# First batch loaded as float32 and cast on chip, denominators ahead of numerators, ordered loads: an attention and feed-forward kernel

## The chip, the cores and the metric

The kernel runs on one core of one Trainium2 chip. The metric is the device time of one execution in microseconds (us); the median of several executions is given. The profile shows one execution; its span, from the first instruction to the last, is 1.7 to 2.0 us shorter than the timed value of the same execution. Engines: TensorE (PE in the profile, with its weight loads as PEld), VectorE (DVE), ScalarE (ACT), GpSimd (POOL) and SP. SP computes nothing and only issues transfers. "ACTq" and "SPq" are the transfers that ScalarE and SP issue.

## The reference

```python
# q, k, v: (8 batches, 8 heads, 576 tokens, 64)
scores = scale * q @ k.T                       # heads 0..3: sliding window of 32
scores = where(masks, scores, -1e9)            # heads 4..7: window of 128, every 4th token
attn = exp(scores - max) / (sum + 1e-9)
x = (attn @ v) laid out as (4608 tokens, 512)
g = x @ w_gate; val = x @ w_val                # 512 -> 1536
out = (gelu(g) * val) @ w_out                  # 1536 -> 512, float32
```

## The kernel before

The feed-forward part goes over 9 chunks of 512 tokens. Each chunk has a first layer (12 blocks of 128 hidden columns, 96 matmuls) and a second half (four tiles of 128 tokens, 48 matmuls, each tile copied and stored). The attention of later batches is woven in. A batch has four units of two heads each (two plain, two dilated): scores on TensorE, an exponential on ScalarE, a mask on VectorE, products with v ("numerators") and with ones ("denominators") on TensorE, then a normalisation in four VectorE steps (transpose, reciprocal, transpose, product into `xT`).

```python
# all q, k, v and weights: casting transfers (float32 -> float16) issued by GpSimd
def load_qk(b):                                   # 14 transfers on GpSimd ...
    for kb in range(5):
        for t, src in ((0, q), (1, k)):
            nc.gpsimd.dma_start(out=qp[0:n, kb, t], in_=...)
    # ... then 7 transposes by DMA, on SP
    nc.sync.dma_start_transpose(out=dst[...], in_=...)
...
# head: batch 0, numerators and denominators of a unit together
for i in range(1, 4):
    emit_s(i, SB, pe_mask=True)
    pv_all(i - 1, 1)                              # products, then the four VectorE steps
pv_all(3, 1)
...
# chunk 0's second half does the scores of batches 1 and 2 and the products of batch 1;
# chunk c from 1 on does the products of batch c+1 and the scores of batch c+2
...
def store(c, tb, bank, eng):
    nc.scalar.activation(osb, ps[:, bank, :], AF.Copy, ...)   # or VectorE
    nc.scalar.dma_start(out=out[t0 : t0 + P, :], in_=osb)     # every store: issued by ScalarE
```

The softmax here doesn't subtract the row's maximum and nothing guards it: scores larger than these inputs give would overflow.

## Time and profile before

| | before |
|---|---|
| time, median (3 runs) | 375.63 us (374.6 to 377.14) |
| span of the profile | 372.9 us, mean granted TensorE clock 0.972 |
| head, to the first first-layer matmul that had to wait | 37.1 us |
| chunk 0: first layer, second half | 21.5 and 26.8 us |
| chunk 1, chunk 2 | 38.9 and 37.0 us |
| the rest | 211.6 us |

The rest is TensorE back to back and moves in no run of this study by more than a microsecond unless a wait lies in it. So, such waits apart, only the first 161 us can gain or lose. The lines behind the table are in the prediction. A line of a timeline has: start, length, engine, line of the program, operation, result<-operands, how many, and in brackets the idle time of the engine before it with what ended that.

### The profile page before, as it was taken

How to read it: one execution, taken by the hardware profiler on the slowest of the kernel's cores; microseconds unless marked ns; L12 is line 12 of the kernel's file. 1: busy time of each engine (PE TensorE's matmuls, PEld its weight loads, DVE VectorE, ACT ScalarE, POOL GpSimd, SP SyncE). 2: the span in 40 equal slices, each digit the busy share in tenths (PEclk: the TensorE clock that was granted, in tenths of full speed). 3: DMA queues.
4: the chain of work that ended last, by engine and by line, in shares of the span. 5: the costliest groups of instructions: out<-in, count | busy, mean ns of one | idle time of the engine just before them, and what ended most of it. 6: DMA issues, size and time to landing. Idle time of an engine off the chain costs nothing.

```text
span 372.9 us, 6286 instructions
## 1 busy us (share of the span) xinstructions
PE 341.8 (92%) x2556; PEld 164.5 (44%) x2556; DVE 196.6 (53%) x285; ACT 144.4 (39%) x204; POOL 120.2 (32%) x175
## 2 busy tenths in 40 slices
PE   1664998959999999999999999999999999999996
PEld 0442443534444444444444444444444444444442
DVE  2356233775973497359725972596269603312420
ACT  2441234445236523652364336434642213313321
POOL 7924947759598657239100000000000000000000
PEclk9996799977999999999999999999999999999999
DMA  9999999999999999989417101100110020011002
GB/s 136 149 206 184 166 207 144 218 203 173 169 139 203 173 161 99 155 170 108 45 59 163 21 2 56 58 0 2 58 57 2 0 86 29 0 58 56 0 28 87
DMA packets 113229, 37.55 MB, mean 101 GB/s; under 512 B 88768, under 2 KB 108480, under 8 KB 113200
## 3 DMA queue, kind: packets, MB, share of 16 engines
q0 software_dynamic: 75440, 19.15, 55.1%
q1 hardware_dynamic: 32576, 8.56, 16.2%
q10 hardware_dynamic: 5184, 9.44, 6.9%
q8 instruction: 20, 0.33, 0.4%
q14 instruction: 9, 0.07, 0.1%
HBM read 38.57 MB, written 9.44 MB: 129 GB/s over the span
## 4 chain that ended last, share of the span: by engine, by line
PE 83%; DVE 11%; ACT 2%; DMA 2%; issue 1%; POOL 0%; DVEq 0%; POOLq 0%
PE ps L433 46%; PE ps L444 25%; PE ps L393 7%; DVE xT L416 3%; DVE dt L398 2%; DVE rb L402 2%; PE ps L310 2%; PE ps L293 2%; DMA qm_first<-in_k_dram 2%; DVE u L438 1%; ACT P L296 1%; DVE rc L400 1%; DVE qTp L208 1%; PE ps L282 1%; DVE osb L457 1%
## 5 line engine op out<-in xcount | busy, mean ns | idle before, releaser
L437 ACT ACTIVATE g<-ps 128x512 f16<-128x512 f32 x108 | 64.0, 597 | 143.2 <-PE ps L433 143.2
L433 PE MATMUL ps<-xT,wg 128*128 128x512 f16 x432 | 114.0, 387 | 1.8 <-DVE xT L416 1.8
L433 PE MATMUL ps<-xT,wv 128*128 128x512 f16 x432 | 112.8, 384 | 0.0
L438 DVE SCALAR_TENSOR_TENSOR u<-g,ps 128x512 f16<-128x512 f16 x108 | 73.9, 688 | 71.2 <-PE ps L433 57.3
L444 PE MATMUL ps<-wo,u 128*128 128x512 f16 x432 | 98.4, 380 | 1.2 <-DVE osb L457 1.2
L433 PEld LDWEIGHTS <-wv 128*128 128x128 f16 x432 | 42.7, 99 | 54.7 <-issue 5.0
L433 PEld LDWEIGHTS <-wg 128*128 128x128 f16 x432 | 40.7, 99 | 49.4 <-issue 3.2
L444 PEld LDWEIGHTS <-u 128*128 128x128 f16 x432 | 40.2, 98 | 48.7 <-issue 1.5
L166 POOL DMA_DIRECT2D qp<-in_q_dram x35 | 25.7, 735 | 14.4 <-DMA wg<-in_moe_w_gate_dram 4.1
L166 POOL DMA_DIRECT2D qp<-in_k_dram x35 | 25.8, 736 | 13.9 <-DMA qd<-in_k_dram 4.3
L398 DVE STREAM_TRANSPOSE dt<-ps 128x576 f32<-128x576 f32 x32 | 25.1, 783 | 9.5 <-PE ps L393 6.2
L317 DVE TENSOR_TENSOR P<-P,mask_p 128x1440 f16<-128x1440 f16 x14 | 12.7, 908 | 27.9 <-ACT P L297 27.9
L312 ACT ACTIVATE P<-ps 128x1280 f16<-128x1280 f32 x16 | 19.8, 1237 | 17.7 <-PE ps L310 15.6
L455 ACT ACTIVATE osb<-ps 128x512 f32<-128x512 f32 x26 | 15.5, 597 | 26.2 <-PE ps L444 26.2
L402 DVE STREAM_TRANSPOSE rb<-rc 128x576 f32<-128x576 f32 x32 | 24.9, 778 | 1.1
L189 POOL DMA_DIRECT2D vp<-in_v_dram x32 | 24.2, 792 | 2.6 <-DMA qp<-in_k_dram 1.6
L457 DVE TENSOR_SCALAR osb<-ps 128x512 f32<-128x512 f32 x10 | 6.9, 690 | 31.8 <-PE ps L444 31.8
L317 DVE TENSOR_TENSOR P<-P,mask_d 128x1280 f16<-128x1280 f16 x14 | 11.5, 824 | 17.6 <-ACT P L312 17.6
L296 ACT ACTIVATE P<-ps 128x800 f16<-128x800 f32 x16 | 13.4, 837 | 14.6 <-PE ps L293 14.5
L416 DVE TENSOR_TENSOR xT<-ps,rb 128x576 f16<-128x576 f32 x16 | 18.0, 1124 | 0.1
L393 PE MATMUL ps<-P,ones 128*64 128x64 f16 (+4 forms) x320 | 15.7, 228 | 0.0
L393 PE MATMUL ps<-P,vd 128*64 128x144 f16 x128 | 8.7, 242 | 6.1 <-DVE xT L416 4.4
(61 smaller groups left out, 203.3 us busy)
## 6 DMA issues: line engine op xcount, KB each, us to landing
out_dram<-osb ACTq DMA_DIRECT2D x36, 256.0 KB, 2.0
vp<-in_v_dram POOLq DMA_DIRECT2D x32, 64.0 KB, 4.6
vd<-in_v_dram POOLq DMA_DIRECT2D x8, 256.0 KB, 5.7
qd<-in_q_dram POOLq DMA_DIRECT2D x7, 256.0 KB, 8.3
qd<-in_k_dram POOLq DMA_DIRECT2D x7, 256.0 KB, 9.7
qp<-in_q_dram POOLq DMA_DIRECT2D x28, 64.0 KB, 5.4
qp<-in_k_dram POOLq DMA_DIRECT2D x28, 64.0 KB, 5.5
wg<-in_moe_w_gate_dram POOLq DMA_DIRECT2D x3, 512.0 KB, 10.2
```

The lines of the kernel that those rows point to most:

```text
L166: nc.gpsimd.dma_start(out=qp[0:n, kb, t], in_=src[b, 0:HK, kb * P : kb * P + n, :].rearrange("h p d -> p h d"),)
L189: nc.gpsimd.dma_start(out=vp[:, kb, :, :], in_=v[b, 0:HK, kb * P : (kb + 1) * P, :].rearrange("h p d -> p h d"),)
L312: nc.scalar.activation(pt, ps[:, b0 : b0 + 4, 0:DW], AF.Exp, bias=0.0, scale=scale)
L317: nc.vector.tensor_tensor(pt, pt, mb, ALU.mult)
L393: nc.tensor.matmul(o, lhs, rhs, start=st, stop=True, skip_group_check=True)
L398: nc.vector.transpose(dt.rearrange("p b c -> p (b c)"), den)
L402: nc.vector.transpose(rb.rearrange("p (b c) -> p b c", c=32), bass.AP(tensor=rc.tensor, offset=rc.offset, ap=[rc.ap[0], [1, 18], [0, 32]]),)
L416: nc.vector.tensor_tensor(dst.rearrange("p (i m s) -> p i m s", m=2, s=2), num, rb.rearrange("p (s m i) -> p i m s", s=2, m=2), ALU.mult,)
L433: nc.tensor.matmul(ps[:, b0 + gi, :], w[:, kc, ns], xT[kc][:, tok], start=(kc == 0), stop=(kc == NKC - 1))
L437: nc.scalar.activation(g, ps[:, b0, :], AF.Gelu)
L438: nc.vector.scalar_tensor_tensor(u_t[nb], g, USCALE, ps[:, b0 + 1, :], ALU.mult, ALU.mult)
L444: nc.tensor.matmul(ps[:, bank, :], u_t[fc][:, tb * P : (tb + 1) * P], wo_t[fc // 4][:, fc % 4, :], start=(fc == 0), stop=(fc == NNB - 1),)
```

## The change

It is meant to shorten the head and to take work from GpSimd and from chunk 0. The first batch comes as plain float32 transfers on SP and ScalarE and is cast on chip. The denominators of a unit go ahead of its numerators, and chunk 0's first layer starts on three of the four key chunks (slices of 128 of the 512 input columns, one from each unit of the attention). Batches 1 to 7 load plain q, k, v as float32 through SP, GpSimd casts them, and a staging pool of single buffers takes the place of double ones. Batch 1 is transposed on TensorE. Batch 1's loads are gated on a weight load, that is, made to wait until it has landed, and batch 2's on the last output weights. Batch 2's scores move from chunk 0 to chunk 1.

```diff
-    ldp = ctx.enter_context(tc.tile_pool(name="ldp", bufs=2))
+    ldp = ctx.enter_context(tc.tile_pool(name="ldp", bufs=1))
...
+    def load_qk_plain(b):                      # 10 transfers on SP, float32
+                gated(nc.sync.dma_start(out=st[0:n, kb, t], in_=sr))
+    def cast_qk_plain(b, st):
+        nc.gpsimd.tensor_copy(qp[:, 0:4], st[:, 0:4])
+        nc.gpsimd.tensor_copy(qp[0:64, 4], st[0:64, 4])
...                                             # v: 5 more transfers on SP, 2 casts
+    def load_batch(b):
+        st = load_qk_plain(b)
+        sv = new_v(b)
+        qd, rd = load_qk_dil(b)
+        qp = cast_qk_plain(b, st)
+        v_plain(b, sv, nc.sync)
+        crossbar(b, qp, qd, rd)                # 7 transposes on SP
+        load_v_dil(b)
+        v_cast(b, sv)
...                                             # head, first batch
+    emit_pv(0, V, ("den",))
+    norm_r(0, V)
...
+    emit_pv(1, V, ("den",))
+    norm_r(1, V)
+    emit_pv(0, V, ("num",))
+    norm_x(0, V)
...
+    gate["dma"] = w1
+    st1 = load_qk_plain(1)
+    qp1 = cast_qk_plain(1, st1)                # in GpSimd's order between load_wo(0) ...
+    load_wo(1)                                 # ... and load_wo(1), load_wo(2)
+    wo2 = load_wo(2)
...                                             # chunk 0
+            if c == 0 and nb == 8:
+                t_plain(1, qp1, 4, ("act", "act", "act", "act"))
+            if c == 0 and nb == 10:
+                gate["dma"] = wo2
+                load_batch(2)
```

## The prediction

> **What bounds the kernel now.** I read the slices and groups of the page first, then cut the span into stages, then walked the chain of waits, then looked at the granted clock, the DMA packets and ScalarE's order of work. By stages (from:to, length, busy us of the TensorE, its weight loads, VectorE, ScalarE, GpSimd, clock, DMA, GB/s):
>
> ```profile
> 0.00:37.10 37.10, 17.07 (x228) 11.41 (x229) 17.16 (x27) 12.62 (x16) 23.05 (x37) 0.92 1.29 169
> 37.10:58.60 21.50, 21.50 (x91) 9.25 (x91) 7.57 (x11) 6.61 (x12) 14.54 (x22) 0.90 1.54 188
> 58.60:85.40 26.80, 20.43 (x252) 11.11 (x250) 18.33 (x26) 12.47 (x15) 19.52 (x29) 0.88 1.68 187
> 85.40:124.30 38.90, 38.74 (x297) 18.07 (x294) 23.57 (x34) 18.00 (x24) 32.04 (x47) 0.95 1.79 168
> 161.30:372.90 211.60, 207.23 (x1405) 97.13 (x1402) 106.99 (x155) 78.02 (x115) 13.21 (x19) 1.00 0.23 49
> ```
>
> These are the head (first batch's attention), chunk 0 of the FFN in two halves, chunk 1, and the last stretch. From 124.3 us on TensorE runs back to back: 96 first-layer matmuls take 20.72 us and 48 second-layer ones 10.36 us in the chain, 0.216 us each, and the nine chunks' 279.7 us cannot shrink. Only the first 124.3 us can. There the chain of waits (start, length, what) is the normalisation, one VectorE step after another:
>
> ```profile
> 21.32 0.83 ACT P L296
> 22.16 0.79 DVE dt L398
> 22.97 0.28 DVE rc L400
> 23.27 0.79 DVE rb L402
> 24.08 0.77 DVE xT L413
> 24.89 0.84 PE ps L393 x20
> ...
> 35.91 1.14 DVE xT L416
> 37.09 21.44 PE ps L433 x89
> ```
>
> Four units pass in single file: numerators and denominators on TensorE (0.84), then four VectorE steps, and the next unit's products wait for the last step to free the bank. The clock in the two late stretches:
>
> ```profile
> 31.00:41.30 10.30, 7.04 (x37) 2.96 (x38) 5.06 (x7) 0.77 (x2) 7.19 (x10) 0.50 1.66 164
> 78.80:89.10 10.30, 7.52 (x75) 4.30 (x75) 6.32 (x9) 7.22 (x8) 8.44 (x12) 0.50 1.83 179
> ```
>
> Half speed, each time after some 3 us in which TensorE did little. One more wait, ScalarE's order near the end of chunk 0:
>
> ```profile
> 75.12 0.60 ACT L455 ACTIVATE osb<-ps 128x512 f32<-128x512 f32 x1 [0.80 <-PE ps L444]
> 78.42 0.34 ACTq L459 DMA_DIRECT2D out_dram<-osb  x1
> 78.80 0.84 ACT L296 ACTIVATE P<-ps 128x800 f16<-128x800 f32 x1 [3.08 <-PE ps L293]
> ```
>
> The tile to be stored was ready at 75.72, the store was issued at 78.42. By the program's own list of waits it reuses one of eight completion counters of the hardware queues, and that counter belonged to a transpose of batch 2 that landed at about 78.4. ScalarE waits in order, so everything behind the store waits too.
>
> **What the Trainium skill says.** "TensorE: Matmul & The Clock Gate", Part 1: the clock is at half until a window of about 3.4 us was busy, and falls back after an idle one. The trace agrees: the 0.50 stretches above, the second after a 2.28 us wait. "DMA: Bandwidth & Descriptors", SWDGE vs HWDGE vs iDMA: a casting DMA must come from GpSimd; SP and ScalarE issue plain ones. So float32 loads need a cast on chip. The trace agrees so far as all loads with a cast sit on GpSimd's queue, at some 0.75 us of GpSimd each, 5.9 us to the first landing. "GPSIMD Engine Reference", 3.1 Elementwise: one-input operations run near 1.03 cycles an element at 1.2 GHz. No trace here shows a cast; my estimate from that page is 0.9 us for 128x1024, 1.8 for 128x2048.
>
> **The change, part by part.**
>
> *Head.* Batch 0's plain q and k now come in 64-float rows, 4608 packets of 256 B. In the trace's packet records, 256 B packets of the hardware queue (ident's 128, and those of the transposes) take 18 ns in the median; over 16 engines that is 5.2 us. The first packet moved at 1.7 us, so they land at L = 7.5 to 10; I take 8.5. Before, the first transpose started at 7.20: nothing is gained in arrival. From L: cast 0.4, transposes 0.4, PSUM copy 0.65 (dense now, against 1.30 strided), bias and scores at half clock 1.6, exponentials 0.84 + 0.70, so the first P is there at L + 4.7. But the first denominators stand behind the dilated transposes, which need two GpSimd casts with two weight DMA issues (0.76 each) between them, after the dilated data (about L + 3.7): L + 8.6. From there VectorE is the bound: four times (0.79 + 0.28 + 0.79), two xT of 0.77 and two of 1.14, four small copies of 0.4: about 12.7. Denominators ahead of numerators remove the 0.84 of TensorE and the wait for it from each of three units. The third unit's xT, which frees the bank, ends at about L + 20.7. The first layer now starts with three of the four key chunks, so the last xT is hidden. Effective start of chunk 0: L + 20.3 = 28.8, against 36.4 before (37.09 less three matmuls done). **Gain 7.6.**
>
> *Chunk 0.* First layer 20.7, half clock at its start about 2.6 (before: 37.09 to 41.3 at half speed, 2.1), 52 transposes of batch 1 that moved from DMA to TensorE: 32 at 0.07 and 20 at 0.035, 2.9. The second half drops batch 2's four scores. FFN 10.4 + four scores at 0.44 + four products at 0.8 = 15.3, plus 2.6 at the end where two normalisations (3.0 each) run in series with 12 matmuls beside them: 17.9. Sum 44.4 against 49.0. **Gain 4.6**, if ScalarE is never held.
>
> *ScalarE held by its stores.* In the changed program's order the second store of chunk 0 takes the counter of the third plain transpose of batch 2, the third and fourth store those of q and k loads of batch 3, which SP issues only after all seven transposes of batch 2. Batch 2's loads wait for the last of wo (estimate 49 us from 15.9 us for six weight loads, 8.2 for wo, and the rest at the packet rates), its dilated loads for the transposes of batch 1 on TensorE (53.5). Transposes then run from about 59, at a pace of 2.0, 1.6 and 1.3 each and 3.5 to landing (the uncontended set at 158.7 us). The second store is ready at 62 and freed at about 69; the fourth, at 75. ScalarE's exponentials stand behind them. Worked through, chunk 0 ends 5.1 later. **Loss 0 to 5.1.**
>
> *Chunk 1.* First layer 20.7. Second half: FFN 10.4, eight scores 3.5, four products 3.2 = 17.1; but the last four scores share four banks and each waits for the exponentials of the one before (1.54 or 1.24 + 0.45), 7 us with little on TensorE: 21.9, and then a half clock stretch, 2.6, and about 1 at its start. Sum 46.2 against 38.9, which had only four scores. **Loss 7.3** (before, the same four scores cost this in chunk 0).
>
> *Rest.* Same matmuls, same order: 0. Plain loads go from 15 GpSimd issues a batch to SP, GpSimd casts 5 to 6 us a batch, off the path.
>
> Sum: -7.6 - 4.6 + 7.3 = -4.9 with ScalarE free; +0.2 or, with one more half clock stretch (1.6), +1.8 with ScalarE fully held. I put about half the weight on each: -1.6. Schedules this deliberate usually were tuned on the chip, so I lean 2 us further to the fast side: 372.0.
>
> **Rivals.** (1) ScalarE is held, all of the head's gain turns into a wait for batch 2's transposes: 377. For: the stalled store above, the order of the changed program. Against: the loads may be 5 us earlier than I think. (2) The head is better than worked (TensorE stays warm, loads land at 7.5, casts are quick) and no store is held: 365. For: DMA has less to do early, transposes of batch 1 left it; before, two waits on transposes cost 2.3 us. Against: VectorE's 12.7 us of chain remains. (3) Weights come late: the first weight load moves behind a GpSimd cast, to about 12 us, later ones behind four casts; slow casts of 2 us each would push wg1 and wo: 380. Against: before they went out at 13.2 to 17.6 too, and the layer now needs them at 28.
>
> **Range and chances.** 2% faster is 368.1: 4 us below my value, needing a free ScalarE and one more good turn: 0.32. 2% slower is 383.1, needing a held ScalarE and late weights: 0.13. Within: 0.55. Range 363.5 to 380.5 from rivals 2 and 3.
>
> **What would show it.** First matmul of the first layer near 27 to 29 us, VectorE nearly gapless from about 17; four normalisations spaced 2.7 to 3 us, not 3.6 to 4.6. Chunk 0's first layer ends near 55. A store issue on ScalarE long after its copy, with a score or an exponential late behind it, shows rival 1. Four scores in single file near 115 us and a clock of 0.50 after. From chunk 2 on, 37.0 us a chunk as before. It is wrong if dilated casts or loads hold the first denominators past 20 us, or if a first-layer matmul waits for weights.

## The result

The changed kernel takes 395.23 us (394.32 to 395.46, 4 runs) against 375.94 us for the kernel before in the same rounds. The ratio is 1.0509, with a 95% interval of 1.0469 to 1.055: slower. Ratios here are the mean time of one kernel's fast runs over that of the other's of the same rounds, so they are not quite the ratios of the medians. The spans are 393.5 and 372.9 us.

The stages of the changed kernel, in the same columns as in the prediction (from:to, length, busy us of TensorE, its weight loads, VectorE, ScalarE, GpSimd, clock, DMA, GB/s):

```profile
0.00:31.30 31.30, 21.32 (x233) 12.72 (x234) 15.06 (x33) 11.18 (x14) 13.06 (x21) 0.87 1.05 198
31.30:61.30 30.00, 26.10 (x149) 12.62 (x147) 9.41 (x13) 11.36 (x22) 8.62 (x12) 0.91 1.09 175
61.30:99.30 38.00, 24.20 (x213) 11.37 (x212) 14.98 (x21) 10.62 (x13) 13.22 (x17) 0.78 1.29 201
99.30:141.00 41.70, 37.85 (x334) 19.06 (x334) 19.96 (x29) 21.85 (x30) 10.19 (x15) 0.94 0.98 143
```

The head ends earlier. The next row, chunk 0's first layer, is 8.5 us longer than before (30.0 against 21.5), and in the third row, chunk 0's second half and the start of chunk 1, TensorE is busy 24.2 of 38.0 us at a clock of 0.78.

The head itself does what was meant. VectorE's first step of the four normalisations (`dt`) and the two last products:

```profile
19.69 0.78 DVE L422 STREAM_TRANSPOSE dt<-ps 128x576 f32<-128x576 f32 x1 [0.21 <-PE ps L417]
23.10 0.78 DVE L422 STREAM_TRANSPOSE dt<-ps 128x576 f32<-128x576 f32 x1
26.20 0.78 DVE L422 STREAM_TRANSPOSE dt<-ps 128x576 f32<-128x576 f32 x1 [0.56 <-PE ps L417]
29.30 0.78 DVE L422 STREAM_TRANSPOSE dt<-ps 128x576 f32<-128x576 f32 x1 [0.57 <-PE ps L417]
31.13 2.12 DVE L440 TENSOR_TENSOR xT<-ps,rb 128x576 f16<-128x576 f32 x2
```

They come every 3.1 to 3.4 us; before, the last two stood 4.6 us apart, and the last `xT` ended at 37.04 and not at 33.25.

ScalarE in chunk 0's second half:

```profile
65.23 0.60 ACT L495 ACTIVATE osb<-ps 128x512 f32<-128x512 f32 x1 [0.64 <-PE ps L484]
73.42 0.37 ACTq L499 DMA_DIRECT2D out_dram<-osb  x1
74.16 0.84 ACT L313 ACTIVATE P<-ps 128x800 f16<-128x800 f32 x1 [8.34 <-DMA sv<-in_v_dram]
...
85.41 0.36 ACTq L499 DMA_DIRECT2D out_dram<-osb  x1
85.82 1.24 ACT L329 ACTIVATE P<-ps 128x1280 f16<-128x1280 f32 x1 [9.73 <-DMA qTp<-qp]
```

The tile is ready at 65.83, its store goes out at 73.42, and the exponential behind it starts at 74.16. What ended the wait is a load of v of batch 2, which neither the tile nor the exponential uses. The second store waits 9.73 us for a transpose of batch 2. In the compiled program each of these stores reuses one of eight completion counters that SP's and ScalarE's transfers share, and the user of that counter before it is this load, or this transpose; ScalarE's wait for its landing stands right in front of the store. The third and fourth store wait likewise for a q and a k load of batch 3 and go out at 90.25 and 93.73.

And what the load and the transpose wait for, from the chain of waits that ended last (start, length, what):

```profile
23.28 7.53 DMA wv<-in_moe_w_val_dram
...
37.31 3.98 SPq L180
...
47.23 3.45 DMA sv<-in_v_dram
50.74 0.19 POOL wo L126
...
51.46 7.58 DMA wo<-in_moe_w_out_dram
59.10 0.37 SPq L180
...
69.84 3.69 DMA sv<-in_v_dram
...
78.03 7.30 DMA qTp<-qp
```

From 23 to 85 us the chain has no TensorE in it. A weight load opens the gate for batch 1's loads; they land at about 48; GpSimd, which casts them, can only then issue the last output weights; these open the gate for batch 2's loads; then come its casts, its transposes and the held store. The chain puts the issue of the weights down to a load of v that landed at the same moment. GpSimd's own timeline shows what stood in front of it:

```profile
48.33 1.89 POOL L185 CAST qp<-st 128x2048 f16<-128x2048 f32 x1 [18.97 <-DMA st<-in_k_dram]
50.16 0.61 POOL L186 CAST qp<-st 64x512 f16<-64x512 f32 x1
50.72 1.48 POOL L126 DMA_DIRECT2D wo<-in_moe_w_out_dram  x2
```

TensorE's matmuls wait for no transfer from 30 to 182 us: their waits in the profile's list are for ScalarE, VectorE and GpSimd, the longest 5.99 and 4.86 us, for the two held exponentials.

Three moments of TensorE compare the kernels: S0, the first score in chunk 0 (end of its first layer), S1, the first score in chunk 1, and S2, the issue of chunk 2's first store. S0 and S1 before, then after:

```profile
59.31 0.49 PE L293 MATMUL ps<-qTp 64*128 64x160 f16 x10
111.76 0.49 PE L293 MATMUL ps<-qTp 64*128 64x160 f16 x10
```

```profile
62.01 0.49 PE L310 MATMUL ps<-qTp 64*128 64x160 f16 x10
117.70 0.49 PE L310 MATMUL ps<-qTp 64*128 64x160 f16 x10
```

S2 before, then after:

```profile
152.58 0.34 ACTq L459 DMA_DIRECT2D out_dram<-osb  x1
```

```profile
173.39 0.34 ACTq L499 DMA_DIRECT2D out_dram<-osb  x1
```

| stretch | before | after | after less before |
|---|---|---|---|
| start to S0 | 59.31 | 62.01 | +2.70 |
| S0 to S1 | 52.45 | 55.69 | +3.24 |
| S1 to S2 (152.58 and 173.39) | 40.82 | 55.69 | +14.87 |
| S2 to the end (372.9 and 393.5) | 220.32 | 220.11 | -0.21 |

The table alone misleads about the place of the loss, because the change moved batch 2's scores from the second stretch into the third. The experiments separate this. Each row is read from one execution: in five traces whose programs are the same up to S0 (the changed kernel and the four runs below that only move its stores) S0 lies between 60.26 and 62.91, so the first row is good to about 2.7 us.

### The profile page after: what moved, and what is told of

It is laid out like the page before. It is cut to its first block, busy times and chain, and to the rows that moved or that the text cites. A ratio compares the mean times of both kernels' runs of the same rounds, so it can differ in the third digit from the quotient of the medians.

```text
span 393.5 us, 6470 instructions
## 1 busy us (share of the span) xinstructions
PE 354.8 (90%) x2616; PEld 170.9 (43%) x2616; DVE 195.2 (50%) x289; ACT 149.1 (38%) x215; POOL 66.6 (17%) x89
## 4 chain that ended last, share of the span: by engine, by line
PE 60%; SPq 15%; DMA 12%; DVE 7%; issue 2%; POOL 1%; ACT 1%; ACTq 0%; POOLq 0%; DVEq 0%
PE ps L452 31%; PE ps L484 21%; SPq L180 9%; SPq L214 4%; PE ps L417 3%; DMA sv<-in_v_dram 3%; DMA wo<-in_moe_w_out_dram 2%; DMA wv<-in_moe_w_val_dram 2%; DMA qTp<-qp 2%; DVE xT L440 2%; DVE dt L422 2%; DVE u_all L478 2%; PE ps L327 1%; SPq L168 1%; DVE rb L426 1%
## 5 line engine op out<-in xcount | busy, mean ns | idle before, releaser
L478 DVE SCALAR_TENSOR_TENSOR u_all<-g,ps 128x512 f16<-128x512 f16 x108 | 73.5, 686 | 80.8 <-PE ps L452 65.0
L452 PE MATMUL ps<-xT,wg 128*128 128x512 f16 x408 | 105.7, 382 | 0.1
L452 PE MATMUL ps<-xT,wv 128*128 128x512 f16 x408 | 104.7, 379 | 0.5 <-DVE u_all L478 0.5
L484 PE MATMUL ps<-wo,u_all 128*128 128x512 f16 x432 | 102.1, 391 | 0.0
L484 PEld LDWEIGHTS <-u_all 128*128 128x128 f16 x432 | 41.3, 100 | 50.6 <-issue 5.2
L452 PEld LDWEIGHTS <-wv 128*128 128x128 f16 x408 | 39.9, 98 | 49.2 <-issue 1.4
L452 PEld LDWEIGHTS <-wg 128*128 128x128 f16 x408 | 38.1, 98 | 45.7 <-issue 1.2
L185 POOL CAST qp<-st 128x2048 f16<-128x2048 f32 x7 | 13.2, 1890 | 86.9 <-DMA st<-in_k_dram 63.4
L327 PE MATMUL ps<-qTd 64*128 64x16 f16 (+1 forms) x256 | 9.9, 208 | 14.6 <-ACT P L313 7.4
L440 DVE TENSOR_TENSOR xT<-ps,rb 128x576 f16<-128x576 f32 x16 | 17.9, 1122 | 0.1
L417 PE MATMUL ps<-P,ones 128*64 128x64 f16 (+4 forms) x320 | 15.4, 226 | 1.9 <-DVE xT L437 1.9
L327 PEld LDWEIGHTS <-qTd 64*128 64x128 f16 x256 | 7.5, 100 | 19.6 <-issue 18.5
```

The source lines that it names most:

```text
L327: mm(o, kt[:, k0 : k0 + P], qt[:, q0:q1], start=st, stop=True, skip_group_check=True)
L417: nc.tensor.matmul(o, lhs, rhs, start=st, stop=True, skip_group_check=True)
L440: nc.vector.tensor_tensor(dst.rearrange("p (i m s) -> p i m s", m=2, s=2), num, rb.rearrange("p (s m i) -> p i m s", s=2, m=2), ALU.mult,)
L452: nc.tensor.matmul(ps[:, b0 + gi, :], w[:, kc, ns], xT[kc][:, tok], start=(kc == 0), stop=(kc == NKC - 1))
L478: nc.vector.scalar_tensor_tensor(u_all[:, nb, :], g, USCALE, ps[:, b0 + 1, :], ALU.mult, ALU.mult)
L484: nc.tensor.matmul(ps[:, bank, :], u_all[:, fc, tb * P : (tb + 1) * P], wo_t[fc // 4][:, fc % 4, :], start=(fc == 0), stop=(fc == NNB - 1),)
```

## The experiments

Theory: ScalarE, held by its own stores, is the loss; the stores wait for SP's late stream of loads and transposes. Rivals: TensorE itself lacks the data; the gates make everything late; the weights are late; later chunks lose by themselves. The first and the third are already weak, since TensorE's matmuls wait for no transfer there. The single buffers of the staging pool were not tested alone; in the changed kernel's trace SP waits for GpSimd 1.5 us in all.

Timed runs, each with the kernel before of the same rounds:

| run | us | before | ratio (95%) |
|---|---|---|---|
| stores of chunks 0 to 2 by GpSimd | 396.56 | 374.71 | 1.0569 (1.0523 to 1.0615) |
| no gates | 395.37 | 374.71 | 1.0537 (1.0482 to 1.0593) |
| both | 395.69 | 374.71 | 1.0555 (1.0494 to 1.0615) |
| casting loads for batches 1 to 7 | 385.32 | 374.71 | 1.0286 (1.0225 to 1.0346) |
| stores of chunk 0 by GpSimd | 391.62 | 375.68 | 1.0429 (1.038 to 1.0478) |
| same, numerators with denominators | 394.34 | 375.68 | 1.0481 (1.0426 to 1.0536) |
| same, batch 1 transposed by DMA | 394.93 | 375.68 | 1.0519 (1.0474 to 1.0564) |
| new head, old loop (wrong result) | 381.13 | 375.68 | 1.0139 (1.0089 to 1.019) |
| stores of chunks 0 and 1 by GpSimd | 391.18 | 375.34 | 1.0423 (1.0407 to 1.044) |
| same, idle matmuls | 391.72 | 375.34 | 1.0409 (1.036 to 1.0458) |
| casting loads, chunk 0's stores by GpSimd | 379.46 | 375.34 | 1.0107 (1.0068 to 1.0146) |
| before, stores on SP | 373.77 | 375.34 | 0.9963 (0.9947 to 0.998) |
| v alone by casting loads | 397.09 | 375.60 | 1.0589 (1.053 to 1.0648) |
| changed kernel, all stores on SP | 383.13 | 375.60 | 1.0218 (1.0149 to 1.0287) |
| before, stores on SP, denominators first | 374.15 | 375.60 | 0.9966 (0.9901 to 1.003) |
| same, idle matmuls | 373.23 | 375.60 | 0.9943 (0.9898 to 0.9989) |
| casting loads, all stores on SP | 375.52 | 375.22 | 1.0032 (0.9986 to 1.0079) |
| same, idle matmuls, masks later | 374.66 | 375.22 | 0.9988 (0.9956 to 1.0019) |

### Stores of chunks 0 to 2 by GpSimd

```diff
-        nc.scalar.dma_start(out=out[t0 : t0 + P, :], in_=osb)
+        eng_dma = nc.gpsimd if c <= 2 else nc.scalar
+        eng_dma.dma_start(out=out[t0 : t0 + P, :], in_=osb)
```

> The changed kernel with the stores of chunks 0 to 2 issued by GpSimd, whose transfers count on other completion counters; nothing else moves. If ScalarE was held by its stores, the second half of chunk 0 falls from 38.0 us to 18 to 21, chunk 2 from 40.6 to about 38, no exponential stands behind a store, and the time is 374 to 378 us (0.995 to 1.007 of the kernel before). If instead the loads and transposes themselves are late for TensorE, the second half stays at 35 or more with TensorE waiting for a landing, and the time stays at 392 to 396 us. If the output weights are late, the second half keeps its waits at the first second-layer matmuls: 388 or more.

The time did not move, so as a time this is a miss. The trace shows why. Chunk 0's second half is free of holds: its first score is at 61.22, and chunk 1's at 101.48, 40.3 us later in place of 55.7. Chunk 2 starts at 124.36, where before starts it. Then chunk 3, whose stores are still ScalarE's, gives it all back:

```profile
210.16 0.84 ACT L313 ACTIVATE P<-ps 128x800 f16<-128x800 f32 x1 [17.30 <-DMA qTp<-qp]
```

The hold was not removed, it moved to the first chunk whose stores share the counters: 17.30 us, until a transpose. That the transposes are so late here comes from GpSimd's order, which now has chunk 2's stores ahead of batch 5's dilated loads: GpSimd waits 30.24 us for the first of these tiles and issues the loads at 165.74, and SP waits 26.7 us for one of them. In the run below that leaves chunk 2's stores on ScalarE the same loads go out at 130.01.

### No gates, and both

```diff
-    gate["dma"] = w1
-                gate["dma"] = wo2
```

> The changed kernel without its two gates on the order of loads (batch 1's loads need not wait for the weights, batch 2's not for the last output weights); stores as in the changed kernel, on ScalarE with the same shared counters. If the gates make the chain of loads late and ScalarE's stores inherit that, everything that holds the stores comes 8 to 12 us earlier, chunk 0's second half is 26 to 30 us, and the time is 383 to 388 us. If the gates protect the weights from the loads, the first layer of chunk 0 now waits for wg1, wv1 or later ones, and the time is 395 us or more. If the gates do nothing, 394 to 396.

> Both edits together: no gates, and the stores of chunks 0 to 2 by GpSimd. If the gates cost only through the held stores, this is within 2 us of the run with the stores moved alone. If the early transposes and batch 1 still came late there, it is 2 to 6 us faster than that run (369 to 373). If the gates protect the weights, it is 2 to 6 us slower.

The gates do nothing in either: 395.37 us without them and 395.69 with the stores moved too (the run above: 396.56). Without the gates SP issues batch 1's loads from 21.2 and not from 30.9 us:

```profile
21.20 4.49 SPq L180 DMA_DIRECT2D st<-in_q_dram  x5
25.73 13.43 SPq L180 DMA_DIRECT2D st<-in_k_dram  x5
```

Five issues, which take 2.9 us when nothing holds them, now take 13.43 (8.98 in the changed kernel), and the cast that waits for the data starts at 47.96 against 48.33. "DMA: Bandwidth & Descriptors", Issuing engines are not separate DMA queues, in the Trainium skill says that transfers of all engines run on the same 16 DMA engines and interleave; this trace agrees. Issued 9.7 us earlier, next to the weights, the loads let the cast start 0.4 us earlier, and the weight loads beside them take 11.6 and 14.3 us to land in place of 7.6 and 9.8.

### Casting loads for batches 1 to 7

```diff
-                gated(nc.sync.dma_start(out=st[0:n, kb, t], in_=sr))     # and the casts
+                nc.gpsimd.dma_start(out=qp[0:n, kb, t], in_=sr)          # v likewise; no gates
```

> The changed kernel with plain q, k and v of batches 1 to 7 loaded by casting transfers of GpSimd, as before the change (no float32 loads on SP, no GpSimd casts, no gates); the head and the order in the chunks stay as changed, stores stay on ScalarE. The hardware counters are then shared by transposes and stores alone. If the float32 loads and their place in SP's order are what the stores wait for, chunk 0's second half is 22 to 28 us and the time 378 to 385 us. If the transposes alone hold the stores as much, it stays above 390. If 15 more issues a batch on GpSimd push the weights out, the first layer or the first second-layer matmuls wait for weights, and the time is 385 to 395.

The second half (59.0 to 84.0, 25.0 us) is in the first range, the time, 385.32 us, just above it. One long hold remains, the second store's, 10.47 us until a transpose of batch 2. S0 to S1 is 48.9 us, between 39.4 (no hold, below) and 55.7. So the float32 loads on SP, with their casts and gates, are about 10 us of the loss as long as the stores stay on ScalarE.

### Stores of chunk 0 alone by GpSimd, then of chunks 0 and 1

```diff
-        nc.scalar.dma_start(...)
+        (nc.gpsimd if c == 0 else nc.scalar).dma_start(...)     # second run: c <= 1
```

> The changed kernel with the four stores of chunk 0 alone issued by GpSimd; all later stores stay on ScalarE, the gates stay. If the held stores of chunk 0 are the whole loss, and the run with chunks 0 to 2 moved lost it again only because chunk 2's stores kept batch 5's loads back on GpSimd, chunk 0's second half is 15 to 17 us, chunk 2 starts near 124.4 us as in the kernel before, there is no wait of 15 us near 211, and the time is 374 to 378 us. If something of the changed kernel slows the later chunks whatever the stores do, it stays above 385.

> The changed kernel with the stores of chunks 0 and 1 by GpSimd, later ones on ScalarE. With chunk 0's alone moved, the hold reappeared in chunk 1 (first store held 13 us until a load of batch 4); with chunks 0 to 2 moved, chunk 2's stores kept batch 5's loads back on GpSimd. If the hold is the whole loss, this version has neither: chunk 0's second half 15 to 17 us, chunk 2 starts at 124 to 126, no wait over 2 us on TensorE after that, and the time is 373 to 379 us. If the hold only moves on to chunk 2 once more, chunk 2 takes 45 us or more and the time is 383 to 392.

Both stayed near 391. In the first, chunk 0 is free (S0 to S1 39.4 us) and chunk 1's first store is held; in the second, chunks 0 and 1 are free and chunk 2's first store is held. The first run:

```profile
119.39 0.84 ACT L313 ACTIVATE P<-ps 128x800 f16<-128x800 f32 x1 [13.25 <-DMA st<-in_k_dram]
```

The second:

```profile
167.24 0.84 ACT L313 ACTIVATE P<-ps 128x800 f16<-128x800 f32 x1 [12.60 <-DMA st<-in_k_dram]
```

With the changed kernel and the first run this is a ladder: the hold is in chunk 0, 1, 2 or 3, whichever is the first whose stores share counters with the loads. S2 moves only a little, 173.39, 169.18 and 166.82: the wait for SP's stream is taken once, in whichever chunk first shares counters with it.

### The parts of the head: numerators with denominators again, and batch 1 by DMA

```diff
-    emit_pv(0, V, ("den",)) ... norm_r(0, V) ... emit_pv(0, V, ("num",)); norm_x(0, V)
+    emit_pv(0, V); norm_r(0, V); norm_x(0, V)                     # first run, four units
-    t_plain(1, ...); t_dil(1, ...)
+    crossbar(1, qp1, qd1, rd1)                                    # second run
```

> As the run with chunk 0's stores moved, and with the order of the head undone: numerators and denominators of a unit together again, each followed by its whole normalisation. If denominators ahead of numerators hide 0.84 us of products and the wait for them in each of three units, the first first-layer matmul comes 2.5 to 4 us later and the time is 2.5 to 4 us longer than that run. If VectorE's chain alone sets the pace, under 1 us.

> As the run with chunk 0's stores moved, and batch 1 transposed by DMA again and not on TensorE. TensorE's part (52 transposes, waits for the cast and for ScalarE's copies, about 6 to 8 us in the trace of chunk 0's first layer) goes away. If the transposes by DMA land after the first scores ask for them (cast at 50, seven transposes at 1.3 to 3 us: 62 to 64 against scores at 54), the time is 0 to 5 us longer than that run. If they land in time, it is 4 to 7 us shorter, 369 to 372.

Both stand on the run with chunk 0's stores moved. In the first, the first first-layer matmuls of chunk 0 start at 38.81 and not at 34.27: the order of the products is worth 4.5 us there. The time grew by only 2.7, because chunk 1's hold shrank (TensorE's wait behind it 6.74 us in place of 10.90): whoever arrives later at a hold waits less. In the second, TensorE waited 9.04, 1.77 and 2.94 us for batch 1's transposes at the start of the second half; S0 was at 65.28 in place of 62.91, and the time 3.3 us longer. Batch 1 on TensorE is right as long as its data comes at 48 us.

### New head, old loop

> The head alone: the first batch as in the changed kernel (float32 loads, casts on chip, denominators first), everything from chunk 0 on as before the change (casting loads by GpSimd, transposes by DMA, batches 1 and 2 scored in chunk 0, stores as before). If the head's gain is real and only the chunks lost, first-layer work starts near 32.5 and not 37, and the time is 370 to 373 us. If batch 1 and the output weights, issued later on GpSimd than before, come late for chunk 0, the gain is gone there: 375 to 382.

The result was wrong (relative error 0.93): the old loop did not call the mask function that the new score routine returns, so the masks were left out. The time, 381.13 us with less VectorE work than a right kernel has, is only an indication. The trace shows the second rival: waits of 1.39 and 2.17 us for output weights and 5.67 us for a transpose of batch 2. In the kernel before, GpSimd issued these transfers with no casts of a head ahead of them; that this makes them late here is argued.

### The same with idle matmuls

```diff
+                warm(3, 0)   # between the four scores at the end of chunk 1; also before
+                s_next()     # chunk 0 and at the end of chunk 0
```

> As the run with the stores of chunks 0 and 1 moved, plus 20 idle matmuls of 128x512 in the gaps of TensorE ahead of chunk 0, at the end of chunk 0 and between the four single-file scores at the end of chunk 1, so that its clock does not fall there. If the half-clock stretches (about 31 to 33, 79 to 83, 122 to 130 in the run with chunks 0 to 2 moved) cost what the rows show, some 2 us each, this is 3 to 6 us shorter than that run: 369 to 373. If the idle matmuls stand in the way of real ones as much as they help, within 1 us.

Within 1 us of the run with the stores of chunks 0 and 1 moved (391.72 and 391.18): chunk 2's hold, still 13.20 us, swallows what was saved ahead of it.

### Casting loads with chunk 0's stores by GpSimd

> The run with casting loads of batches 1 to 7 by GpSimd, with chunk 0's stores moved to GpSimd. There the only hold left was chunk 0's second store, 10.5 us until a transpose of batch 2. If that was the rest of that run's loss, this is 9 to 11 us shorter than its 385.3: 374 to 377 us. If the hold moves on to chunk 1 as it did with float32 loads, 383 to 387.

379.46 us, 5.9 less than with casting loads alone and not 9 to 11. No hold over 2 us is left (1.71 us in chunk 2). The hold did not move on: SP now has only seven transposes a batch and is idle from 79.03 to 95.00 and from 105.72 to 122.69 us. With no hold left the time is still 1% above before: the rest of the change is no gain.

### V alone by casting loads

> The changed kernel with plain v alone of batches 1 to 7 loaded by casting transfers of GpSimd: SP issues 17 transfers a batch and not 22, all else stays, stores on ScalarE. If SP's own pace sets when chunk 2's first store can go, each batch takes SP some 3 us less (v's five issues took 2.85), over four batches 8 to 12 us: chunk 2's first store at 162 to 166 and not 173.4, and the time 384 to 388 us, between the changed kernel (395) and the run with all plain loads by GpSimd (385). If the store was held by something else, 393 to 396.

A miss: 397.09 us. SP's q loads of batches 2, 3 and 4 begin at 62.58, 81.98 and 103.79 (59.10, 82.73 and 106.11 in the changed kernel). So the pace is what was expected, 19.4 and 21.8 us a batch in place of 23.6 and 23.4, some 3 us less. But the stream begins 3.5 us later, since v's five issues on GpSimd stand ahead of the output weights that open the gate, and the hold is decided in chunk 0, where only 0.75 us of the gain has come through (81.98 against 82.73): chunk 0's stores are held to 94.30 (93.73). Chunk 2's first store then goes at 173.70 without any hold.

### The changed kernel with all stores on SP

```diff
-        nc.scalar.dma_start(out=out[t0 : t0 + P, :], in_=osb)
+        nc.sync.dma_start(out=out[t0 : t0 + P, :], in_=osb)
```

> The changed kernel with every store on SP. No store holds ScalarE, in any chunk. But a chunk's stores now stand ahead of the loads of the next batch on SP, which takes 22 us for a batch's loads and transposes, while the scores ask for them 21 to 25 us into the chunk. If SP's pace is the limit, TensorE now waits for transposes, 3 to 5 us in each of chunks 2 to 5, and the time is 383 to 391 us. If the coupling of ScalarE to the loads was the whole loss, 374 to 378.

383.13 us: 3% less than the changed kernel, by one word. No exponential waits for a transfer in any chunk. S0 to S1 is 39.4 us and S2 is 156.41, 17.0 us earlier than in the changed kernel. Whether it is still 2% slower than before is unclear by the interval (1.0149 to 1.0287). From S2 on it loses about 3 us, as SP's order now puts stores ahead of loads and TensorE waits for transposes (1.03 us at 191 and 1.07 at 229 us; the rest of the 3 was not followed).

### The kernel before: stores on SP, denominators first, idle matmuls

```diff
-        nc.scalar.dma_start(...)                     +        nc.sync.dma_start(...)          # first run
-        pv_all(i - 1, 1)                             +  den, norm_r, num, norm_x as changed  # second
+                warm(4, 0)                           # third: behind the last scores of chunk 0
```

> The kernel before with all stores on SP, behind the transposes of the batch loaded in the same chunk, instead of on ScalarE. ScalarE's hold of 2.7 us in chunk 0 goes away. If a transposes' lateness alone set the pace there, the scores of batch 2 wait as long and the time is within 1 us of before; if the hold was the cost, 2 to 3 us shorter, 372 to 373.5. If stores on SP keep transposes back, longer.

> The kernel before with stores on SP (0.996 of before in an earlier run) and of the change only this: denominators ahead of numerators for the first batch, and the first layer of chunk 0 started on three of its four key chunks. Undone in the changed kernel, the order of the head cost 4.5 us at the first first-layer matmul (38.8 against 34.3). If it pays as much here, first-layer work starts near 33 and not 37 and the time is 369 to 372 us (0.985 to 0.99). If chunk 0 then waits for batch 2's transposes or the output weights, which come no earlier, 372 to 374.

> As the run before it, with four idle matmuls of 128x512 behind each of the last scores of chunk 0, which stand in single file and leave the clock at half from 78.8 to 89.1 in the kernel before. In the changed kernel's chunk 1 such matmuls saved 2.0 us by the trace. If the same holds here: 1 to 2.5 us shorter than the run before it. If they stand in the way, 0 to 1 longer.

The first is 0.4% faster than before. With denominators first, first-layer work starts at 32.26, and the third block of the first layer at 37.67 and not at 41.95: 4.3 us. That is most of the changed kernel's own 5.9 (36.05), with the old loads. But the gain then goes: 1.38 us of waiting for output weights and

```profile
79.84 0.52 PE L293 MATMUL ps<-qTp 64*128 64x80 f16 x6 [5.52 <-DMA qTp<-qp]
```

for batch 2's last transpose, which comes no earlier. The time is level with the run before it. With idle matmuls the clock stays up (1.00 from 85.4 to 124.3, against 0.94) and the median is 373.23, the shortest; its interval just lies below 1, and against the run before it the difference is not settled.

### Casting loads and all stores on SP

> The changed kernel with plain q, k and v of batches 1 to 7 by casting transfers of GpSimd, and every store on SP behind the transposes: no store can hold ScalarE, and SP has seven transposes a batch and the stores. With casting loads and chunk 0's stores on GpSimd, 379.5 us with one hold of 1.7 us left. If the rest of the change (new head, batch 1 on TensorE, the order in the chunks) comes out level with before, 375 to 379 us here, chunk 1 starting near 76 and chunk 2 near 123. If stores on SP keep the transposes late, TensorE waits for them in chunks 2 to 5 and it is 380 or more.

> As the run before it, with idle matmuls between the four single-file scores at the end of chunk 1, and three of batch 3's four masks moved on VectorE from the start of chunk 2 to behind its later blocks. With all stores on SP, TensorE waited 2.75 us at the start of chunk 2 for VectorE, which had 5.3 us of masks in front, and the clock was at 0.61 and 0.88 just before and after. If these two are chunk 2's own loss, this is 3 to 5 us shorter than the run before it: 371 to 375. If they hide behind something else, within 1 us.

The first takes away the float32 loads of batches 1 to 7, their gates and every hold, and keeps the rest of the change. It is level with before, 1.0032. Its S0 and S1:

```profile
59.75 0.49 PE L314 MATMUL ps<-qTp 64*128 64x160 f16 x10
99.15 0.49 PE L314 MATMUL ps<-qTp 64*128 64x160 f16 x10
```

S2 is 153.10. Against before: S0 +0.4 us, S0 to S1 -13.05, S1 to S2 +13.1. The batch's scores that moved from chunk 0 to chunk 1 cost about as much there as they saved (2.7 us of the 13.1 lie in chunk 2, see below). The second run treats chunks 1 and 2 (idle matmuls between the single-file scores, three masks later) and gains 0.9 us by the medians, not 3 to 5: S2 comes only 0.8 us earlier. With both, the change is at the level of before and no better.

## Why the prediction was wrong, point by point

**Head: right in kind, 1.2 us off.** Predicted effective start 28.8; by it the third first-layer block would begin at 34.9 (28.8, 16 matmuls at 0.216, 2.6 of half clock); measured 36.05. The normalisations came 3.1 to 3.4 us apart, just above the 2.7 to 3 said. Most of the head's gain belongs to the order of the products and the start on three key chunks: the kernel before with these alone has 4.3 of the 5.9 us.

**Chunk 0's first layer: a term was missing.** From the third block to S0 the prediction has 20.1 us (20.7 less the 16 matmuls, plus 2.9 for batch 1's transposes), the trace 25.96. The 2.9 counted the transposes alone. Around them TensorE waited 1.98 us for GpSimd's cast of batch 1 and twice 0.94 us or more for ScalarE's PSUM copies, and the clock fell to 0.52 from 50.4 to 53.8. "Gain 4.6" for chunk 0 unheld was so eaten before its second half began: S0 is 59.75 in the run without holds (casting loads, all stores on SP), not 55.0. The second half there took 15.4 us (59.75 to 75.20), less than the 17.9 predicted. (The prediction's own parts for chunk 0 add to 44.1 and not to the 44.4 it gives; that changes nothing.)

**ScalarE held by its stores: the mechanism was right, its size was not.** This is the step that failed. "Loss 0 to 5.1" measures 16.3: S0 to S1 is 39.4 us in four runs without the hold (chunk 0's stores by GpSimd or all stores on SP, each with float32 and with casting loads) and 55.7 with it. Three inputs of that step were off. The first store was left out and was held 8.34 us. The second was to be freed at about 69 and was at 85.41, the fourth at 75 and was at 93.73. Most of that comes from the estimate of 49 us for the last output weights, with transposes from 59: the weights landed at 59.0 and the transposes began at 70.68. The transpose that frees the second store then took 7.30 us to land and not 3.5. The estimate added up transfers at their packet rates and left out that GpSimd issues these weights only behind its cast of batch 1, whose loads land at 48. The run without gates shows that issuing batch 1's loads earlier would not have helped: the DMA engines were taken, at 188 to 199 GB/s from 20 to 45 us. Issuing these weights ahead of the cast was not tried. "DMA: Bandwidth & Descriptors", Anatomy of one DMA — SWDGE (gpsimd) path, in the Trainium skill says that a semaphore wait of a transfer happens on the issuing sequencer, before dispatch. The trace agrees, with a number: everything of ScalarE behind one store stood 8.34 and 9.73 us.

**Half the weight on each.** The prediction mixed "free" and "held" evenly. The compiled program names, for each of the four stores, the transfer of a later batch that it waits for. The only question was when those land, so the held value should have had most of the weight.

**Chunk 1: near.** Predicted 46.2 us; without the hold 75.20 to 122.04, 46.8. Chunk 2 was said to stay at 37.0; without holds the way from its start to its first store takes 31.1 us against 28.4 (start 124.18 before), 2.7 more. The half clock is not most of it: in the run with idle matmuls and later masks, at a clock of 1.00, it is still 30.7 (from 121.66), and TensorE waits 0.90, 0.53 and 0.89 us for VectorE's products.

**The lean of 2 us to the fast side** "because such schedules usually were tuned on the chip" had no line behind it, and was in the wrong direction.

**Rivals.** Rival 1, held ScalarE, was the right one, at 377 us in place of 395. Rival 3, late weights, is in the chain (wo at 51.46 to 59.04), not as a wait of TensorE but as the reason why the stream of loads is late.

**The sum.** By the trace, the hold of 16.3 us in chunk 0 and 2.15 in chunk 2 are 18.5 of the 20.6 us between the spans. By experiment the hold and the loads are not apart so cleanly. The medians are 395.23 us as changed, 383.13 with all stores on SP, 385.32 with casting loads and 375.52 with both: moving the stores alone recovers 12.1 us, and the other 7.6 go only with the float32 loads. The rest of the change comes out level, 1.0032, so with ScalarE free the prediction's gain of 4.9 us was not there either; S0 came 4.7 us later than predicted. SP's pace of some 23 us a batch (59.10, 82.73, 106.11) is the time of its own 22 issues, one behind the other: no gap between the rows of its timeline from 59 to 106 us is over 0.25 us. One transfer for four blocks of rows, to make them fewer, could not be built (too many dimensions), so it was not tried.

## What to carry to other kernels

A transfer issued by a compute engine makes everything behind it wait for whatever its completion counter waits for, and with counters shared among queues that can be a load for a later batch on another engine: look up, for each store, who used its counter last, and put stores on a queue that computes nothing, after a look at what will stand behind them there (on GpSimd four stores kept batch 5's loads back). Removing such a wait in one place moves it to the next place that has it, so remove the coupling and not the instance. And a gain at the start is only a gain if the data that the next stage needs comes earlier too; here the head's 4 to 6 us were given back each time as a wait for batch 1 or 2.

## What the Trainium skill lacked or had wrong

- No page says that stores of ScalarE and loads of SP can wait for each other through shared completion counters ("DMA: Bandwidth & Descriptors" would be the place). Here such waits took 8.34, 9.73, 13.25, 12.60 and 17.30 us, each in front of an exponential that needed none of the data.
- "DMA: Bandwidth & Descriptors", Issuing engines are not separate DMA queues, is right and could carry a number: loads issued 9.7 us earlier beside weight loads let their cast start 0.4 us earlier. It does not say that an issue itself takes longer beside other transfers: five took 13.43 us in place of 2.9.
- "GPSIMD Engine Reference", 3.1 Elementwise, gives 1.03 cycles per element, which the prediction took for one-input operations, and no time for what an operation costs on top. The casts measure 1.04 us for 128x1024 and 1.89 us for 128x2048: by the difference 0.85 us for 1024 elements, 1.0 cycle each at the page's 1.2 GHz, and about 0.2 us on top each time; the prediction's 0.9 and 1.8 were short by 0.1.
- "TensorE: Matmul & The Clock Gate", Part 1, gives two clocks, half and full, and a window of about 3.4 us; that holds here (0.50 to 0.52 in five stretches of the changed kernel, 3.4, 3.4, 10.2, 6.9 and 6.9 us long). What it does not say is what idle matmuls are worth when something else waits. In two pairs of runs (in the second, masks moved too) they brought the clock from 85.4 to 124.3 us from 0.94 and 0.91 to 1.00 and the median down by 0.9 us, which the intervals do not settle, and by nothing where a hold stood behind them.
